# Attention with a fused feed-forward layer on one Trainium2 core: one softmax pass without a maximum, exponentials of 1536 columns, and an order of instructions made by a list scheduler

## The chip, the core and the metric

The kernel runs on one core of one Trainium2 chip. The metric is the device time of one execution in microseconds (us), from the first to the last instruction. Times that are compared come from the same call on the same chip unless the text says otherwise.

The kernels use five engines of the core. Each runs its own list of instructions, and they wait for one another at semaphores: TensorE (PE: matmuls; PEld: its weight loads), VectorE (DVE), ScalarE (ACT), GpSimd (POOL) and SyncE (SP, which issues the DMAs here). Matmul results land in PSUM, which the kernels use as 8 banks of 512 fp32 columns.

## The reference

```python
# S = 2048 tokens, D = 512, H = 32 heads of 16, F = 1792; all bf16
xn  = layernorm(x)
qkv = xn @ wqkv                                  # -> q, k, v per head
p   = softmax(q @ k.T * 0.25, axis=-1)           # 32 heads, 2048 x 2048 scores each
att = (p @ v) @ wo
ffn = (silu(xn @ w1) * (xn @ w3)) @ w2
out = x + att + ffn
```

Together the 32 heads have 32 x 2048 x 2048 scores. On 128 partitions that is 2048 tiles of 128 x 512, and every element of them goes through an exponential. ScalarE computes them all.

## The kernel before

The work is cut into 32 units: 4 blocks of 512 queries times 8 groups of 4 heads. Each unit is passed over twice. Pass 1 computes scores with queries on the partitions, and VectorE takes their maximum. The negated maximum is put into two spare rows of the query tile. Pass 2 computes the transposed scores, now shifted by the maximum, and ScalarE exponentiates them. A period of the program ("burst") holds two score matmuls of each pass:

```python
for i in range(2):                      # pass 1: banks 0..2 in turn
    b = (2 * p1 + i) % 3
    P.op("dve", lambda e: e.tensor_reduce(part[...], bank(b), AX.X, ALU.max), ...)
for i in range(2):                      # pass 2: banks 3..5 in turn, one 512-wide exp each
    r = 2 * p2 + i; b = 3 + r % 3
    P.op("act", lambda e: e.activation(PT[:, r % NPT, :], bank(b), ACTF.Exp, scale=SCALE), ...)
```

`PT` (exponentials, bf16) is multiplied with the values, which carry a column of ones, so bank 7 collects the weighted values and the row sums. Projections and the feed-forward layer ("dense tiles": 4 matmuls of 32 output columns side by side, called a group below) go through bank 6 in the remaining time. ScalarE copies nearly every dense result out of PSUM, in halves of 256 columns. Where a period has no dense group left, a filler multiplies zero weights into bank 7:

```python
if k == 0 and n < NB:
    filler(n)
```

## Time and profile before

| | |
|---|---|
| time, median of 3 | 1415.93 us (1413.53 to 1416.27) |
| VectorE busy | 1302.4 us, 92% |
| ScalarE busy | 1268.4 us, 89% |
| TensorE busy | 1042.1 us, 73% |
| granted TensorE clock, mean | 0.943 of full speed |

These lines of the page of the kernel before give the span, each engine's busy time with its share of the span and number of instructions, and the busy tenths in 40 equal slices; PEclk is the granted clock in tenths.

```profile
span 1417.8 us, 31821 instructions
PE 1042.1 (73%) x12357; PEld 270.8 (19%) x12357; DVE 1302.4 (92%) x2176; ACT 1268.4 (89%) x2709; POOL 251.0 (18%) x335
...
DVE  5999999999999999999999999999999999999801
ACT  4689999999999999989999999999999999999982
...
PEclk9998899999999999979999999999999999999998
...
DVE 42%; ACT 28%; PE 22%; issue 3%; POOL 2%; DMA 1%; SPq 0%; POOLq 0%; ACTq 0%; DVEq 0%
DVE part L778 42%; ACT PT L801 22%; PE ps L771 10%; PE ps L355 10%; PE ps L816 2%; ACT zg L374 1%; ACT QT L372 1%; ACT KT L390 1%; ACT ub L372 1%; ACT th L372 1%; PE ps L656 1%; DMA R<-Rrow 1%; ACT xnT L334 1%; POOL a L463 0%; ACT osb L372 0%
...
L778 DVE TENSOR_REDUCE part<-ps 128x1 f32<-128x512 f32 x2048 | 1267.3, 683 | 32.9 <-PE ps L771 21.6
L801 ACT ACTIVATE PT<-ps 128x512 bf16<-128x512 f32 x2048 | 1134.4, 619 | 87.0 <-PE ps L771 47.5
L771 PE MATMUL ps<-KT,QT 32*128 32x512 bf16 x2048 | 419.8, 403 | 288.9 <-DVE part L778 245.0
```

The two lines of percentages are the chain that ended last, by engine and by line. A group's line ends with its busy time, the mean duration of one in ns, and the idle time of its engine before it with what ended most of that. The reader should see two engines near 90%, a chain that changes sides between them, and a TensorE that waits 245 us for the reduction.

One more line is from the timeline of ScalarE near the end, where only pass 2 still runs (start, duration, engine, line, what, count):

```profile
1358.02 32.01 ACT L801 ACTIVATE PT<-ps 128x512 bf16<-128x512 f32 x58 [0.65 <-PE ps L771]
```

58 exponentials in 32.01 us are 0.552 us each. The line shows a wait of 0.65 us before the first of them and no gap between them.

### The profile page before, as it was taken

The page shows a single profiled execution, that of the slowest core. Times are in us where ns is not written, and L with a number is a line of the kernel's source. Part 1 is how long each engine was busy: PE and PEld are TensorE (multiplying, and loading weights), DVE is VectorE, ACT ScalarE, POOL GpSimd, SP SyncE. Part 2 cuts the span into 40 slices and gives each one's busy share as a digit, 9 for nine tenths or more (in the row PEclk, how much of TensorE's full clock was granted, in tenths as well). Part 3 has the DMA queues.
Part 4 walks back from the last instruction along what each step waited for, and adds up shares of the span by engine and source line. Part 5 has one row for each costly group of instructions (what it writes and reads, how often), then busy time and mean ns, then how long its engine had stood idle before and what let it go on. Part 6 is the DMA issues. An engine that isn't in the chain of part 4 may idle for free.

```text
span 1417.8 us, 31821 instructions
## 1 busy us (share of the span) xinstructions
PE 1042.1 (73%) x12357; PEld 270.8 (19%) x12357; DVE 1302.4 (92%) x2176; ACT 1268.4 (89%) x2709; POOL 251.0 (18%) x335
## 2 busy tenths in 40 slices
PE   4987777777777777777776777776777777777795
PEld 2321111111111111111111111111111111111121
DVE  5999999999999999999999999999999999999801
ACT  4689999999999999989999999999999999999982
POOL 5241010012122100112222011112221111112200
PEclk9998899999999999979999999999999999999998
DMA  9100111111111111110111111111111111011111
GB/s 215 28 12 4 11 6 13 6 13 20 18 19 13 17 17 17 18 20 16 21 20 21 17 17 17 5 29 20 21 21 20 17 17 6 13 25 20 6 6 20
DMA packets 80724, 29.85 MB, mean 21 GB/s; under 512 B 70336, under 2 KB 78528, under 8 KB 80576
## 3 DMA queue, kind: packets, MB, share of 16 engines
q1 hardware_dynamic: 80576, 27.81, 15.6%
q8 instruction: 101, 1.65, 0.5%
q14 instruction: 47, 0.39, 0.1%
HBM read 20.71 MB, written 2.10 MB: 16 GB/s over the span
## 4 chain that ended last, share of the span: by engine, by line
DVE 42%; ACT 28%; PE 22%; issue 3%; POOL 2%; DMA 1%; SPq 0%; POOLq 0%; ACTq 0%; DVEq 0%
DVE part L778 42%; ACT PT L801 22%; PE ps L771 10%; PE ps L355 10%; PE ps L816 2%; ACT zg L374 1%; ACT QT L372 1%; ACT KT L390 1%; ACT ub L372 1%; ACT th L372 1%; PE ps L656 1%; DMA R<-Rrow 1%; ACT xnT L334 1%; POOL a L463 0%; ACT osb L372 0%
## 5 line engine op out<-in xcount | busy, mean ns | idle before, releaser
L778 DVE TENSOR_REDUCE part<-ps 128x1 f32<-128x512 f32 x2048 | 1267.3, 683 | 32.9 <-PE ps L771 21.6
L801 ACT ACTIVATE PT<-ps 128x512 bf16<-128x512 f32 x2048 | 1134.4, 619 | 87.0 <-PE ps L771 47.5
L771 PE MATMUL ps<-KT,QT 32*128 32x512 bf16 x2048 | 419.8, 403 | 288.9 <-DVE part L778 245.0
L771 PE MATMUL ps<-QT,KT 32*128 32x512 bf16 x2048 | 418.4, 405 | 3.8 <-ACT PT L801 3.8
L771 PEld LDWEIGHTS ps<-KT,QT 32*128 32x128 bf16 x2048 | 107.4, 91 | 744.1 <-DVE part L778 743.2
L816 PE MATMUL ps<-PT,Vaug 128*17 128x512 bf16 x2048 | 211.7, 404 | 8.8 <-ACT U L372 8.4
L355 PE MATMUL ps<-xnT,w 128*32 128x512 bf16 x1792 | 162.2, 409 | 29.6 <-ACT QT L372 10.8
L656 PE MATMUL ps<-KT,zeros_t 128*17 128x512 bf16 x1400 | 138.3, 400 | 0.0
L771 PEld LDWEIGHTS ps<-QT,KT 32*128 32x128 bf16 x2048 | 96.9, 91 | 21.6 <-ACT PT L801 21.6
L463 POOL TENSOR_TENSOR a<-zg,ub 128x512 f32<-128x512 bf16 x56 | 64.7, 1155 | 75.7 <-ACT ub L372 75.5
L816 PEld LDWEIGHTS ps<-PT,Vaug 128*17 128x17 bf16 x2048 | 49.6, 87 | 138.2 <-issue 119.8
L786 POOL TENSOR_SCALAR negm<-mfin 128x16 f32<-128x16 f32 x32 | 6.6, 205 | 383.1 <-DVE mfin L783 383.1
L355 PE MATMUL ps<-w,hT 128*32 128x512 bf16 x896 | 73.5, 393 | 0.0
L465 POOL TENSOR_TENSOR hT<-a,t 128x512 bf16<-128x512 f32 x56 | 71.1, 1269 | 4.4
L461 POOL TENSOR_SCALAR t<-th 128x512 f32<-128x512 bf16 x56 | 34.8, 621 | 194.8 <-ACT th L372 193.8
L856 POOL TENSOR_TENSOR wk_on<-U,R 128x512 bf16<-128x512 f32 x16 | 20.3, 1268 | 256.7 <-DMA R<-Rrow 232.8
L856 POOL TENSOR_TENSOR on_b<-U,R 128x512 bf16<-128x512 f32 x16 | 20.3, 1270 | 225.9 <-DMA R<-Rrow 150.1
L355 PEld LDWEIGHTS ps<-xnT,w 128*32 128x32 bf16 x1792 | 39.8, 95 | 88.2 <-issue 81.8
L355 PE MATMUL ps<-xnT,wk_on 128*32 128x512 bf16 x512 | 50.0, 453 | 8.8 <-ACT xnT L334 3.6
L372 ACT ACTIVATE th<-zg 128x256 bf16<-128x256 bf16 x112 | 51.5, 460 | 0.5
L374 ACT ACTIVATE zg<-ps 128x256 bf16<-128x256 f32 x112 | 46.4, 414 | 3.7 <-PE ps L355 2.3
L355 PE MATMUL ps<-xnT,wq 128*32 128x512 bf16 x512 | 45.5, 396 | 3.6 <-ACT zg L374 3.6
(64 smaller groups left out, 475.1 us busy)
## 6 DMA issues: line engine op xcount, KB each, us to landing
w<-in_B_w_dram SPq DMA_DIRECT2D x112, 128.0 KB, 2.4
R<-Rrow SPq DMA_DIRECT2D x128, 32.0 KB, 3.4
x_sb<-in_A_x_dram SPq DMA_DIRECT2D x4, 512.0 KB, 7.9
out_dram<-osb SPq DMA_DIRECT2D x16, 128.0 KB
w<-in_B_w_dram SPq DMA_DIRECT2D x1, 1792.0 KB
hT<-in_A_wqkv_dram SPq DMA_DIRECT2D x3, 512.0 KB
QT<-Zs SPq DMA_DIRECT2D x64, 4.0 KB
wo<-in_A_wo_dram SPq DMA_DIRECT2D x4, 128.0 KB
```

Source lines behind the costliest of these rows:

```text
L355: ins = e.matmul(bank(bk)[32 * i:32 * i + 32, 0:ncols], make_lhsT(i), rhs_ap, start=start, stop=stop, tile_position=(0, 32 * i))
L372: P.op("act", lambda e: e.activation(dst_fn(h), src_fn(h), func), reads=reads, writes=writes)
L374: P.op("act", lambda e: e.activation(dst_fn(h), src_fn(h), func, scale=scale), reads=reads, writes=writes)
L461: P.op("pool", lambda e: e.tensor_scalar(t1[:, :], th[:, ss, :], 1.0, 1.0, ALU.mult, ALU.add), reads=[("th", ss)], writes=[("t1",)])
L463: P.op("pool", lambda e: e.tensor_tensor(a32[:, :], zg[:, ss, :], ub[:, ss, :], ALU.mult), reads=[("zg", ss), ("ub", ss)], writes=[("a32",)])
L465: P.op("pool", lambda e: e.tensor_tensor(hT[:, sc % 2, fc, :], a32[:, :], t1[:, :], ALU.mult), reads=[("a32",), ("t1",)], writes=[("hT", s ...
L656: ins = e.matmul(bank(7)[32 * j:32 * j + 17, :], zeros_t[:, 0:17], KT[:, 0, 0:512], start=False, stop=False, skip_group_check=True, tile_p ...
L771: ins = e.matmul(bank(b), lhsT, rhs, start=True, stop=True, tile_position=(rp, 0))
L778: P.op("dve", lambda e, qt=qt, j=j, kc=kc, b=b: e.tensor_reduce(part[:, qt, j, kc:kc + 1], bank(b), AX.X, ALU.max), reads=[("ps", b)], wri ...
L801: P.op("act", lambda e, b=b, r=r: e.activation(PT[:, r % NPT, :], bank(b), ACTF.Exp, scale=SCALE), reads=[("ps", b)], writes=[("PT", r % N ...
L816: ins = e.matmul(bank(7)[32 * j:32 * j + 17, :], Vaug[:, ktq, 4 * gq + j, :], PT[:, rj[j] % NPT, :], start=(ktq == 0), stop=(ktq == NT - 1 ...
L856: P.op("pool", lambda e: e.tensor_tensor(onorm[ob][:, gq, :], U[:, us, :], R[:, :], ALU.mult), reads=[("U", us)] + [("R", j_) for j_ in ra ...
```

## The change

Intent: drop the maximum, since the scores are small, and with it the whole first pass; make ScalarE's exponentials as wide as three banks; give ScalarE's copies to VectorE; and let a list scheduler, which runs at build time with a duration for each instruction, fix the order on every engine. The old two-pass program stays as a second program. On the chip the row sums are compared with 2^-20 and 2^60 and the value weights with 2^40; if the test fails, every engine runs the old program after the new one.

The core of the diff, with cuts marked:

```diff
+_LAT = 0.09
+class _Sched(_Prog):                     # list scheduler: op(..., dur=) has a modelled end
+    def op(self, eng, fn, reads=(), writes=(), dur=0.1, name=""):
+        op = _Prog.op(self, eng, fn, reads, writes, name)
+        return self._time(op, op.deps, dur, 0.18 if eng == "pe" else 0.0)
+    ...
+        a_cost = lambda n: 0.113 + 0.000835 * n      # ScalarE, n columns
+        d_cost = lambda n: 0.095 + 0.00104 * n       # VectorE
+    DG = 0.24                                        # four dense matmuls on TensorE
+    ...
+        def norm(t):
+            xs = t % 4
+            o = P.op("dve", lambda e: e.tensor_scalar(xn_sb[:, xs, :], x_sb[:, t, :], ...
+    ...
+            def emit():                              # w = 3 banks, two such buffers
+                q = P.op("act", lambda e: e.activation(
+                    PT[:, s0:s0 + w, :].rearrange("p a b -> p (a b)"),
+                    ps[:, 3 * buf * 512:(3 * buf + w) * 512],
+                    ACTF.Exp, scale=SCALE),
+                    reads=wr, writes=[("PT", r % NSL) for r in rs], dur=a_cost(512 * w))
+    ...
+                    elif try_score() or try_pv() or try_dense():     # TensorE's priorities
+                        moved = True
+    ...
+            reg = e.alloc_register("slow_" + name)
+            e.reg_load(reg, flag[0:1, 0:1])
+            with e.If(e.snap(reg) > 0):
+                ...
+                PM.emit_engine(name, e, sems[1][0], sems[1][1])     # the old program
```

The fast program has no fillers. Its exponentials number 683 (682 of 1536 columns and one of 1024). Scores have two buffers, banks 0 to 2 and 3 to 5; bank 6 takes dense tiles and bank 7 the value sums. Until the inputs are ready ("early") only the first score buffer is used.

## The prediction

> **What bounds the kernel now.** The page gives VectorE 92% busy, ScalarE 89%, TensorE 73% of a 1417.8 us span. The chain of waits runs 42% through the max reduction, 28% through ScalarE, 22% through TensorE. The groups view has 2048 reductions, 1267 us, and 2048 exponentials of 512 columns, 1134 us; around them ScalarE copies nearly every PSUM result (about 270 us). Two nearly full engines take turns as the limit, and one in-order TensorE feeds both: it waits 245 us for the reduction.
>
> **Removed.** All of pass 1: 2048 score matmuls and reductions, the max transposes with their copies and DMAs, 1400 filler matmuls. ScalarE's copies and GpSimd's gate products go to VectorE. VectorE falls from 1302 to about 170 us (some 240 operations of 0.62 us, plus norms), TensorE from 12357 matmuls to about 8600.
>
> **Left on ScalarE, the new bound.** In the tail of the old timeline, where only pass 2 runs, 58 exponentials take 32.0 us: 0.552 us for 512 columns. The Trainium skill ("ScalarE: Activation LUTs", What ACT_TABLE_LOAD costs) gives 0.833 ns per element and a fixed part; this trace agrees (256 columns 0.41 us, 512 columns 0.62 us, each alone). So 1536 columns should take 0.552 + 1024 x 0.833 ns = 1.405 us; 683 of them, 960 us. Widening alone is worth 170 us against 2048 x 0.552. Add 56 tanh, 31 us, and 14 transposed-input copies, 8 us.
>
> **Around it (estimates from durations in this trace).**
> - Start: first exponential at about 18 us (first burst now at 32).
> - Early phase: one score buffer, so some 20 exponentials also wait about 0.6 us for their scores: 12 us.
> - Tail: last values, three DMA hops for the division (the last took 6.5 us to land here), four short output tiles, output DMA: 20 us, against 27 now. The check mostly hides under it: 2 us.
> - Stalls where the static order differs from the chip: about 25 us.
>
> Sum: 960 + 31 + 8 + 18 + 12 + 20 + 2 + 25, about 1075; I shade it to 1065, since a timed list scheduler made the order. Row sums are far inside the check's limits (scores of standard deviation near 1.3 over 2048 keys), so the fallback is not run.
>
> **Prediction: 1065 us, range 1030 to 1115. Faster by over 2%: 0.97; within 2%: 0.01; slower: 0.02** (only if the fallback runs, near 2400 us).
>
> **What would show each step.** ScalarE at 93% or more of the span; one group of 683 exponentials at about 1.40 us per step; the chain of waits over 75% in them; VectorE under 20% busy; TensorE 60 to 70%; ScalarE's idle time before exponentials, released by TensorE, 20 to 50 us in all.
>
> **What would make it wrong.** (1) Without fillers TensorE's granted clock (0.943 now) may drop in stretches that hold only scores and values, as the skill ("TensorE: Matmul & The Clock Gate", Part 1) warns of idle. Slow bursts in this trace take 0.61 instead of 0.39 us, a dense group 0.43 instead of 0.22. Scores alone still fit into 1.4 us; interleaved with dense tiles they would not, and ScalarE would starve: I expect a mean clock of 0.75 to 0.95. A clock near 0.5 throughout would cost 50 us or more. (2) A read across three PSUM banks may be slower than linear. (3) The single bank for dense tiles may hold TensorE behind a late evacuation, and so the next scores. (4) The dense work of a quarter waits for the last division of the quarter before, so it may pile up at the end.

## The result, and the profile after

| | before | after |
|---|---|---|
| time, median | 1416.01 us (4 runs) | 1023.31 us (4 runs, 1019.11 to 1024.02) |
| ratio | | 0.7225, 95% interval 0.7208 to 0.7242 |
| VectorE busy | 1302.4 us, 92% | 203.1 us, 20% |
| ScalarE busy | 1268.4 us, 89% | 959.1 us, 94% |
| TensorE busy | 1042.1 us, 73% | 803.3 us, 79% |
| mean granted clock | 0.943 | 0.824 |

The time lies below the predicted range (1030 to 1115 us). The output is correct.

These are the same lines of the page of the changed kernel.

```profile
span 1022.1 us, 19380 instructions
PE 803.3 (79%) x8641; PEld 221.6 (22%) x8641; DVE 203.1 (20%) x347; ACT 959.1 (94%) x755; POOL 61.0 (6%) x81
...
DVE  7742233310001222100001222200001122210012
ACT  2799999999999999999999999999999999999991
...
PEclk9999999975579999855559999955558999975578
...
ACT 77%; PE 15%; DVE 3%; DMA 2%; issue 2%; SPq 0%; DVEq 0%
ACT f_PT L1464 74%; PE ps L1192 9%; PE ps L1454 4%; ACT f_th L1291 3%; PE ps L1491 2%; DMA f_wv<-in_A_wqkv_dram 1%; DVE f_KT L1203 1%; DMA f_Lc<-f_U 1%; DVE f_hT L1305 0%; DMA f_R<-f_Rrow 0%; DVE f_xn_sb L1096 0%; DVE f_t L1295 0%; PE ps L1214 0%; DVE f_QT L1203 0%; DVE f_osb L1352 0%
...
L1464 ACT ACTIVATE f_PT<-ps 128x1536 bf16<-128x1536 f32 (+1 forms) x683 | 940.6, 1661 | 24.2 <-PE ps L1454 24.0
L1454 PE MATMUL ps<-f_QT,f_KT 32*128 32x512 bf16 x2048 | 319.6, 462 | 139.5 <-ACT f_PT L1464 136.1
```

The chain now runs through ScalarE, with 24 us of idle time before exponentials that scores ended. The clock has long stretches at half speed, marked 5 in PEclk. (The mean of 1661 ns is no step: the record of an exponential may start while the one before still runs. Steps must be taken from ends.)

The ends of consecutive exponentials, taken one by one from the two traces, give this table. It holds only pairs with nothing else between them on ScalarE.

```
kernel, exponentials                  pairs   step, us (number of pairs)
before, 512 wide, all                 1508    0.488 to 0.492 (1024 pairs); the rest mostly 0.69 to 0.71 (311) and 0.76 (65)
before, 512 wide, after 1358 us         57    0.488 and 0.612 in turn; mean 0.551
after, 1536 wide                       621    1.340 to 1.345 (589 pairs); median 1.343
```

This table is where the prediction failed. The 0.552 us is the mean of a step that ScalarE takes by itself (0.488) and one in which it waits for scores (0.612), because two exponentials share one burst of scores and three banks don't let the next burst start in time. The score matmuls of the old tail (TensorE's timeline) show it:

```profile
1359.77 0.39 PE L771 MATMUL ps<-QT,KT 32*128 32x512 bf16 x2 [0.71 <-ACT PT L801]
...
1360.87 0.39 PE L771 MATMUL ps<-QT,KT 32*128 32x512 bf16 x2
...
1361.97 0.39 PE L771 MATMUL ps<-QT,KT 32*128 32x512 bf16 x2 [0.16 <-ACT PT L801]
...
1363.07 0.39 PE L771 MATMUL ps<-QT,KT 32*128 32x512 bf16 x2
```

A burst comes every 1.10 us, which is 0.488 + 0.612. In the trace the burst at 1360.87 starts 0.05 us after an exponential has ended at 1360.82, so it waited for that bank. The first exponential on its scores is released only at 1361.29, just as the exponential before ends at 1361.30. The timeline of ScalarE shows no gap because records overlap: an exponential that doesn't wait starts 0.10 us before the one before ends, and one that waits starts 0.015 us after it. ScalarE's own step is 0.488 us for 512 columns and 1.343 us for 1536. The line through these two has 0.835 ns per column and 0.061 us fixed, half of the 0.125 us that the prediction carried into every one of the 683.

The largest part of the steady idle time looks like this. It is the timeline of the changed kernel around a query tile at half clock.

```profile
257.15 0.61 PE L1454 MATMUL ps<-f_QT,f_KT 32*128 32x512 bf16 x3 [0.20 <-ACT f_PT L1464]
...
257.69 0.61 PE L1491 MATMUL ps<-f_PT,f_Vaug 128*17 128x512 bf16 x4
...
258.09 1.92 PE L1192 MATMUL ps<-f_xnT,f_wq 128*32 128x512 bf16 x16
...
259.94 1.03 PE L1454 MATMUL ps<-f_QT,f_KT 32*128 32x512 bf16 x6
...
260.60 4.13 ACT L1464 ACTIVATE f_PT<-ps 128x1536 bf16<-128x1536 f32 x3 [0.81 <-PE ps L1454]
```

The four groups of the query tile (16 matmuls) take 1.92 us, where the scheduler allowed 4 x 0.24. The next scores stand behind them, and ScalarE starves for 0.8 us. Over the steady part (53 to 1001 us) ScalarE idles 15.9 us in all.

The start and the early phase hold the rest. These lines are VectorE and GpSimd just before and after the first exponential.

```profile
20.26 4.09 DVE L1096 TENSOR_SCALAR f_xn_sb<-f_x_sb,f_lnr,f_lnb 128x512 bf16<-128x512 bf16 x2
...
20.37 3.51 POOL L1142 MEMSET f_wo<- 128x4096 bf16 x1
```

Two normalisations that take 0.7 us together elsewhere take 4.09 us while GpSimd clears the output weights; the first alone takes 3.77 us. The Trainium skill ("SBUF — State Buffer", SBUF: two separate sides) says that VectorE in some modes and GpSimd hold a common pair of ports exclusively for a whole instruction. The trace agrees: the first normalisation ends 0.15 us after the 3.51 us of the clearing, and the second follows at its normal 0.39 us. (The record of the first starts 0.11 us before that of the clearing, so these records don't tell which of the two got the ports first.)

### The profile page after: what moved, and what is told of

Read it like the earlier page. It is cut to its first block, busy times and chain, and to the rows that moved or that the text cites. A ratio compares the mean times of both kernels' runs of the same rounds, so it can differ in the third digit from the quotient of the medians.

```text
span 1022.1 us, 19380 instructions
## 1 busy us (share of the span) xinstructions
PE 803.3 (79%) x8641; PEld 221.6 (22%) x8641; DVE 203.1 (20%) x347; ACT 959.1 (94%) x755; POOL 61.0 (6%) x81
## 3 DMA queue, kind: packets, MB, share of 16 engines
q1 hardware_dynamic: 80080, 27.54, 21.5%
## 4 chain that ended last, share of the span: by engine, by line
ACT 77%; PE 15%; DVE 3%; DMA 2%; issue 2%; SPq 0%; DVEq 0%
ACT f_PT L1464 74%; PE ps L1192 9%; PE ps L1454 4%; ACT f_th L1291 3%; PE ps L1491 2%; DMA f_wv<-in_A_wqkv_dram 1%; DVE f_KT L1203 1%; DMA f_Lc<-f_U 1%; DVE f_hT L1305 0%; DMA f_R<-f_Rrow 0%; DVE f_xn_sb L1096 0%; DVE f_t L1295 0%; PE ps L1214 0%; DVE f_QT L1203 0%; DVE f_osb L1352 0%
## 5 line engine op out<-in xcount | busy, mean ns | idle before, releaser
L1464 ACT ACTIVATE f_PT<-ps 128x1536 bf16<-128x1536 f32 (+1 forms) x683 | 940.6, 1661 | 24.2 <-PE ps L1454 24.0
L1454 PE MATMUL ps<-f_QT,f_KT 32*128 32x512 bf16 x2048 | 319.6, 462 | 139.5 <-ACT f_PT L1464 136.1
L1491 PE MATMUL ps<-f_PT,f_Vaug 128*17 128x512 bf16 x2048 | 239.7, 459 | 0.7 <-DVE f_U L1508 0.7
L1454 PEld LDWEIGHTS ps<-f_QT,f_KT 32*128 32x128 bf16 x2048 | 68.6, 94 | 434.8 <-ACT f_PT L1464 387.9
L1192 PE MATMUL ps<-f_xnT,f_w 128*32 128x512 bf16 x1792 | 129.3, 381 | 38.8 <-DVE f_t L1295 26.6
L1491 PEld LDWEIGHTS ps<-f_PT,f_Vaug 128*17 128x17 bf16 x2048 | 50.1, 88 | 156.6 <-issue 148.6
L1192 PE MATMUL ps<-f_w,f_hT 128*32 128x512 bf16 x896 | 64.8, 398 | 2.8 <-DVE f_osb L1352 1.6
L1192 PEld LDWEIGHTS ps<-f_xnT,f_w 128*32 128x32 bf16 x1792 | 42.7, 95 | 86.9 <-issue 61.2
L1192 PE MATMUL ps<-f_xnT,f_wq 128*32 128x512 bf16 x512 | 47.0, 484 | 7.2 <-DVE f_t L1295 5.6
L1291 ACT ACTIVATE f_th<-ps 128x512 f32<-128x512 f32 x56 | 49.2, 878 | 1.4 <-PE ps L1192 1.4
```

Of the source, the lines that this page charges most:

```text
L1192: ins = e.matmul(bank(bk)[32 * i:32 * i + 32, 0:ncols], make_lhsT(i), rhs_ap, start=start, stop=stop, tile_position=(0, 32 * i))
L1291: q = P.op("act", lambda e: e.activation(th[:, ss, :], bank(bk), ACTF.Tanh, scale=0.5), reads=[("ps", bk)], writes=[("th", ss)], dur=a_cos ...
L1454: ins = e.matmul(bank(b), l_, r_, start=True, stop=True, tile_position=(rp, 0))
L1464: q = P.op("act", lambda e: e.activation(PT[:, s0:s0 + w, :].rearrange("p a b -> p (a b)"), ps[:, 3 * buf * 512:(3 * buf + w) * 512], ACTF ...
L1491: ins = e.matmul(bank(PV)[32 * j:32 * j + 17, :], Vaug[:, kt, 4 * g + j, :], PT[:, (4 * m + j) % NSL, :], start=(kt == 0), stop=(kt == NT ...
```

## The experiments

The theories at the start were these.
- A: the step of an exponential was mis-sized, because its fixed part is 0.061 us. The rival R1 keeps 0.125 us and gives another reason for cheap wide reads.
- B: the steady stalls come from query tiles at half clock.
- C: the start is late because value tiles block TensorE.
- D and E, formed later, are about where the rest of the gain comes from.

The ratios are against the kernel before.

### Width of the exponential

exp_512 and exp_768 cut each exponential into three or two.

```diff
-  q = P.op("act", lambda e: e.activation(PT[.., s0:s0+w, ..], ps[three banks], Exp),
-           reads=wr, writes=[("PT", r % NSL) for r in rs], dur=a_cost(512 * w))
+  for h in range(3):                     # exp_768: range(2), 768 columns
+      q = P.op("act", lambda e, h=h: e.activation(PTf[:, h*step:(h+1)*step], ps[...], Exp),
+               reads=wr, writes=[("PT", r % NSL) for r in rs], dur=a_cost(step))
```

> The changed kernel with every 1536-wide exponential cut into three of 512 columns; scores, order and buffers stay. Theory A (the fixed part of one exponential is about 62 ns, read from back-to-back steps of 0.488 us for 512 columns in the old trace and 1.343 us for 1536 in the new one; the prediction's 0.552 us came from a stretch where ScalarE also waited for scores): 1365 more instructions x 62 ns = +85 us, about 1108 us. Rival R1 (the fixed part is 125 ns, as the prediction took, and a wide read over three banks is cheaper for another reason): +170 us, about 1193 us.

> The same with two exponentials of 768 columns (the cut lies inside a bank). Theory A: 683 x 62 ns = +42 us, about 1065 us, step 0.70 us. Rival R1: +85 us, about 1108 us. If only the number of instructions counts, exp_512 adds twice what this adds.

Measured: exp_512 1284.78 us (ratio 0.9068) with a wrong result; exp_768 1154.51 us (0.8153), correct. Both are far slower than either theory allowed. Their steps show why: exp_512 has 592 steps of 0.488 us and 1365 of 0.629 us; exp_768 has 572 of 0.700 to 0.702 and 682 of about 0.842 us. 1365 and 682 are the numbers of pieces that follow another piece of the same exponential. My edit named all three banks and slots for each piece, so the program made each piece wait for ScalarE's own semaphore of the piece before, and that wait costs 0.141 us. Steps without it are 0.488 and 0.701 us, and 0.701 - 256 x 0.835 ns is 0.487: one line through all three widths.

The wrong result has its own cause. A replay of the order in which the build emits operations shows it: the normalised input tiles have four slots, and `norm(t)` has no condition that the transpose of tile t - 4 was emitted. In the change only the modelled times keep that order. With the slower exponentials, tile 13 was emitted before the transpose of tile 9. The trace of exp_512 agrees: that normalisation starts at 34.9 us, and the transpose of tile 9 ends at 35.8. The check for races sees nothing, since every access waits for the one emitted before it.

exp_512_free mends both: exact banks and slots, and conditions for reused slots.

```diff
-  P.post("dve", lambda t=t: norm(t), ready=..., prio=1)
+  P.post("dve", lambda t=t: norm(t), ready=..., prio=1,
+         cond=lambda t=t: t < 4 or ("TR", t - 4) in done)
+  # the same for the copies U and R of the division of unit u - 2 and u - 1
+  for h in range(w):
+      q = P.op("act", ... PT[:, s0 + h, :], bank 3*buf+h ..., reads=[wr[h]], writes=[("PT", s0 + h)])
```

> exp_512 once more, with two mistakes of that run mended: each 512-wide exponential names only its own bank and its own slot, so that none waits on its own engine for the one before (two of three did, at 0.629 us a step against 0.488), and the normalised input tiles and the divisions wait for the slot they overwrite, which the change itself leaves to the modelled times. Result correct. Theory A: 1365 more instructions x 61 ns = +83 us over 1022, 1100 to 1112 us, all steps near 0.488. Rival R1: +170 us. If it is still wrong, the order of the input tiles was not the cause.

Measured: 1102.03 us (ratio 0.7794, interval 0.7776 to 0.7812), correct; 1950 of 1986 steps are 0.488 to 0.492 us. That is 80 us above the changed kernel (1020 to 1023 us), against 83 by theory A and 170 by R1. R1 is out. Widening is worth 80 us, not the 170 us of the prediction.

### Copies back on ScalarE, and the fallback by force

copies_act moves the copies of keys, queries and values to ScalarE; forced_fallback sets `L_HI = 2.0 ** 4`, so that the check must fail.

> The changed kernel with the copies of keys, queries and values (80 tiles of 512 columns) put back from VectorE to ScalarE. If ScalarE is the bound through nearly the whole span, each copy adds its step of 0.49 us: +39 us, less a few for the 21 early ones that fall into ScalarE's idle time: 1050 to 1062 us. Rival (the limit is the handoff of scores by TensorE): ScalarE has room, below +10 us.

> The upper limit of the row-sum check lowered to 16, so the check fails on purpose and the two-pass program runs after the fast one. The result stays correct and the time is near the sum of both, 1022 + 1416 = 2440 us. If the check were not wired to the branch, the time would stay at 1022 us.

Measured: copies_act 1047.29 us (0.7400), about 25 us more than the changed kernel and a little under the expected range. ScalarE's share rose to 96%. Of 561 steps between exponentials 556 stayed at 1.343 us; the copies of the early phase fell into idle time, and the stalls at query tiles shrank from 0.92 to 0.38 us, which the expectation had left out. So ScalarE is the bound through most of the span: of the 39 us of steps given to it (80 x 0.49), about 25 were paid, and the rest went into idle time that was there before (24 of the 80 copies start before 53 us). The result was wrong for the reason above: the replay shows tiles 12 to 15 emitted before the transposes of 8 to 11, and the trace has the same order. The work is the same.

forced_fallback took 2426.9 us in one run and was correct. The check is wired to the branch, and failing it costs about the sum of both programs (1022 + 1416 = 2438 us).

### Stalls and clock

slow_dense sets `DG = 0.45`; fillers adds zero-weight matmuls wherever the schedule leaves TensorE idle.

```diff
   elif try_score() or try_pv() or try_dense():
       moved = True
+  elif not st["early"] and st["sc"] < NGR and pvb[0] <= P.t and st["pv"] % NT:
+      ...   # four matmuls, zero weights, added to the open sums in bank 7, dur=0.24
```

> The changed kernel once more, as the yardstick for the small effects of this call: 1019 to 1024 us, ratio 0.7225.

> The scheduler is told that a dense group of four matmuls takes 0.45 us instead of 0.24. Theory B (the 15 or so stalls of 0.9 us in the steady part come from the four groups of a query tile, which take 1.9 us at half clock in front of the next scores, where the schedule allowed 0.96): the groups are spread over two or more exponentials, the stalls go, -10 to -15 us, with the clock still low (about 0.8). Rival B2 (the stalls come from the low clock itself, whatever the order): no change within 3 us.

> Filler matmuls (zero weights added to the open value sums) where the schedule leaves TensorE idle, to hold the clock up. Theory B: clock above 0.95, query tiles take 1.05 us, the stalls of 0.9 us go, -10 to -15 us, unless the fillers themselves stand in front of scores. Rival B2 says the same here; so this run with slow_dense tells order from clock. If the clock costs nothing anywhere: no change or slower.

Measured: after_again 1020.13 us (0.7217); slow_dense 1030.75 us (0.7281), wrong result; fillers 1011.39 us (0.7148, interval 0.7132 to 0.7164), correct.

slow_dense doesn't tell order from clock. Its clock rose to 0.904, where about 0.8 was expected. The constant also slowed the early phase (first exponential at 27.6 us instead of 21.1) and left one stall of 6.9 us at 76.8 us, where scores stood behind several tiles of keys and queries in a row; and at query tiles stalls of 0.51 and some 0.2 us remained, since two groups still fit between scores in the model. Its result is wrong because tiles 12 to 15 overtook again, and because in the replay a division's factors were overwritten by the next unit's before use (in the trace the load of the next factors is issued before the multiplication at 3 of 32 units). Fillers held the clock at 0.993, and the stalls of 0.9 us were gone. The gain was 9 us, a little less than expected, because fillers themselves now stood before scores and left many stalls of 0.12 to 0.18 us. The trace agrees with the gain: ScalarE's stalls after 53 us, counted beyond each instruction's own step, fell from 14.9 us in after_again to 5.8. So the low clock cost about 1% here, through the query tiles. Whether another order would have avoided these stalls at the low clock is not shown. This is PEclk of fillers:

```profile
PEclk9999999999999999999999999999999999999997
```

### The start

v_late lets value tiles begin only after the first scores.

```diff
-  crit = [(0, i, x) for i, x in enumerate(order)]
+  crit = [(1 if x.name[0] == "V" else 0, i, x) for i, x in enumerate(order)]
```

> Value tiles may start only after the first group of scores is issued. In the trace TensorE stands at 12 us waiting for the load of the value weights, with the transposes of input tiles 2 and 3 behind two cold value tiles, and the first exponential starts at 20.8 us. Theory C: the first exponential comes 5 us or so earlier, and the whole gains 2 to 5 us. Rival (the early phase is bound by VectorE and TensorE together until 53 us): the first exponential comes earlier, the end does not move, within 2 us.

Measured: 1019.62 us (0.7202) against 1020.13. The first exponential came at 16.2 us instead of 21.1, and the end did not move. The rival holds: until about 53 us other things bound the early phase (the 4.09 us above are still there).

### Where the rest of the gain comes from

one_pass_old is the kernel before with pass 1 and the maximum taken out. one_pass_old_dve moves its copies to VectorE too.

```diff
-  p1 = n if n < NPB else None
+  p1 = None                    # no pass 1, so no maximum and no shift
-  LAG = BU + 8
+  LAG = 28
-  assert ("QTP", u2) in done, ...
+  assert ("QT", u2) in done and ("KT", g2, kt // 4) in done, ...
+  # one_pass_old_dve only:  evac_on_dve = [True]
```

> The kernel before with pass 1 and the maximum taken out and nothing else: 512-wide exponentials, three score banks, the old order by periods, copies on ScalarE. Theory D (ScalarE and its handoff take over at once as the bound): 1024 pairs at 0.488 + 0.611 us as in the old tail, 1126 us, plus copies of 256 columns that do not fit into the handoff waits, about 120 us, plus start 70 and tail 27 us: about 1340 us, a gain of only 75 us although VectorE loses 1267 us of work. Rival (the reductions were the bound by themselves): about 1200 us or less.

> The same with the copies moved from ScalarE to VectorE (all but those of the keys). Theory D: 1126 + tanh 30 + start 70 + tail 27 us, about 1255 us; what then is left to the changed kernel (about 230 us) is the width of the exponentials with double-buffered groups of three banks, and the start. If the handoff were not the limit, 2048 x 0.488 = 1000 us would show instead: about 1130 us.

Measured: one_pass_old **1487.92 us**, ratio 1.0544, so slower than the kernel before although VectorE lost 1267 us of work; one_pass_old_dve 1379.43 us (0.9749). Theory D fell. The clock was 0.663 and 0.753. This is the stretch from 400 to 440 us of one_pass_old (columns: stretch, length, busy time and count of PE, PEld, DVE, ACT and POOL, granted clock, DMA share, GB/s):

```profile
400.00:440.00 40.00, 37.21 (x244) 6.37 (x240) 0.25 (x1) 34.77 (x75) 9.75 (x9) 0.54 0.17 21
```

TensorE is busy 37.2 of 40 us, yet it completes only 244 matmuls, and its clock stays at half. In the same stretch the kernel before does more matmuls in less time:

```profile
400.00:440.00 40.00, 29.04 (x332) 7.25 (x328) 38.90 (x65) 38.09 (x85) 8.10 (x10) 0.91 0.16 19
```

To tell the clock from the handoff, one_pass_warm and one_pass_dve_warm add work: they keep the two score matmuls of pass 1 in each period, into banks that nobody reads.

```diff
-  if p1 is None and n >= NPB + 2:        # the old kernel did this in its tail only
+  if p2 is not None:
       for i in range(2):
           mms.append((i, KT[32*j:32*j+32, 0, 0:128], KT[32*j:32*j+32, 0, 0:512], 32*j))
```

> one_pass_old with two more score matmuls in every period, into banks that nobody reads, so that TensorE's work is as in the kernel before but no reduction waits on it. Theory E (the low clock made one_pass_old slow: at half clock TensorE is full): clock above 0.9, 1320 to 1370 us. Rival E2 (the handoff over three banks and the copies on ScalarE cost it, whatever the clock): more work for TensorE makes it no faster, 1480 us or more.

> The same for one_pass_old_dve. Theory E: clock above 0.9, 1240 to 1280 us, the pair of exponentials stepping 0.488 + 0.611 us. Rival E2: about 1380 us.

Measured: one_pass_warm **1330.30 us** (0.9399), one_pass_dve_warm 1265.84 us (0.8946), both correct, with clocks of 0.963 and 0.973. 2048 useless matmuls made the kernels 158 and 114 us faster. The same stretch of one_pass_warm:

```profile
400.00:440.00 40.00, 32.15 (x392) 7.34 (x388) 0.25 (x1) 38.47 (x77) 1.85 (x2) 0.96 0.11 9
```

392 matmuls now take less time than 244 did. Theory E holds for both. In one_pass_dve_warm 1024 steps between exponentials are 0.488 us and 829 of the other 869 are 0.61 us, the handoff again. With the clock held up, theory D's sums (1340 and 1255 us) come within 11 us of what is measured; the clock was what they had left out.

So the gain divides into steps. The first two were measured at a clock of 0.96 and 0.97, the last two at 0.81 and 0.82; holding the clock of the changed kernel up with fillers gave 9 us more. The sizes hold for this order of the steps. They are differences of medians of different calls, whose medians of the kernel before differ by under 4 us:

```
                                                          us      gain
kernel before                                           1415
one pass, TensorE kept warm        (one_pass_warm)      1330        85
copies (not of keys) to VectorE    (one_pass_dve_warm)  1266        64
list order, double-buffered scores (exp_512_free)       1102       164
exponentials of 1536 columns       (after)              1022        80
```

The "one pass" of the title gives 85 us of 393, and by itself in the old order it gives less than nothing. The largest step is the one in which ScalarE no longer waits for its scores: 829 steps of 0.61 us that become 0.488 are worth about 829 x 0.12 = 100 us of it (an estimate from the steps above). The two traces divide the 164 us further: the first exponential starts at 64.7 us in one_pass_dve_warm and at 21.9 in exp_512_free, which is 43 us; the tail after the last one is 7 us shorter; and the stretch from the first exponential to the last is 115 us shorter. No run separates the double buffer from the list order.

### The check

> The changed kernel without the flag's register loads, branches and second program (the flag is still computed). By the prediction 2 us faster, 1018 to 1020 us where the full one has 1020 to 1023; if the branch and the last waits hide nothing, 3 to 5 us faster.

> The changed kernel again, as the yardstick for no_check on the same chip: 1019 to 1024 us.

Measured: no_check 1018.76 us (0.7206, interval 0.7181 to 0.7230), after_third 1023.47 us (0.7236, interval 0.7214 to 0.7258). The intervals of the ratios overlap, but their five times don't overlap: 1016.71 to 1021.67 us against 1022.69 to 1024.45, with means 4.3 us apart. The traces give the place. From the end of the last exponential to the end of the span no_check takes 18.5 us, and the three profiles of the changed kernel 21.5, 21.6 and 22.4. So the check costs 3 to 4 us and not 2.

In the trace of the changed kernel the flag is written at 1005.0 us, long before the end. SyncE loads it at 1017.7, after its last output DMA, and its branch ends at 1018.4. The last output data have landed at 1019.4, but SyncE's waits for the DMA semaphores begin only at 1020.9, 2.5 us after the branch, and follow one by one until 1021.7. In no_check they begin 0.05 us after the last output DMA is issued. TensorE's branch alone takes 3.9 us, ending at 1018.7, before SyncE is done.

### A faster version

best_b takes what the runs taught: fillers only where the modelled exponential has 0.7 us left, the true cost of an exponential in the scheduler, late value tiles, early copies on ScalarE where it is idle, the clearing of the output weights at 70 us, and the missing conditions.

```diff
-  a_cost = lambda n: 0.113 + 0.000835 * n
+  a_cost = lambda n: 0.061 + 0.000835 * n
+  elif ... P.free["act"] > P.t + 0.7 ...: filler
```

> The changed kernel with: fillers only where the modelled exponential still has 0.7 us to run; the exponential's cost in the scheduler corrected to 0.061 us + 0.835 ns per column; value tiles after the first scores; the clearing of the output weights on GpSimd moved from 20 us to 70 us, since in the trace two normalisations on VectorE took 4.09 us under it instead of 0.7; early copies on ScalarE where it is idle; and the missing waits for the overwritten slots. Stalls of 15 us in the steady part and 3 to 8 us of the early phase go: 995 to 1008 us, correct. If the small stalls in front of scores seen with fillers stay, about 1008 to 1012 us.

Measured: **999.83 us** (996.97 to 1000.35, ratio 0.7072, interval 0.7057 to 0.7086), correct. These are lines of its page.

```profile
span 998.6 us, 23622 instructions
PE 836.3 (84%) x10765; PEld 238.5 (24%) x10765; DVE 194.7 (19%) x339; ACT 960.4 (96%) x763; POOL 61.4 (6%) x82
...
PEclk9999999999999999999899999999989999998998
...
ACT 91%; PE 4%; issue 2%; DMA 1%; DVE 1%; SPq 0%; POOL 0%; DVEq 0%
```

Between its first exponential and the last, ScalarE loses about 6 us beyond the instructions' own steps, against about 29 us in the changed kernel. From VectorE's timeline, two normalisations take their normal time again:

```profile
18.83 0.73 DVE L1099 TENSOR_SCALAR f_xn_sb<-f_x_sb,f_lnr,f_lnb 128x512 bf16<-128x512 bf16 x2
```

The parts of best_b were not measured one by one, apart from fillers (in another form) and v_late. v_late still has the 4.09 us, so moving the clearing is what removed them.

## Why the prediction was right or wrong

The predicted sum, before it was shaded to 1065, against what the trace of the changed kernel has (stalls are counted beyond each instruction's own step from end to end, which adds about 0.1 us per stall to the gaps between records):

| term of the prediction | predicted, us | measured, us |
|---|---|---|
| 683 exponentials | 960 | 917 (683 x 1.343) |
| 56 tanh | 31 | 27 (56 x 0.489) |
| 14 input copies | 8 | 7 |
| first exponential at | 18 | 20.8 |
| early waits and stalls | 12 + 25 | about 29 (10 before 53 us, 19 after) |
| tail and check | 20 + 2 | 21.5 |
| sum | 1075 | 1022 |

**What failed.** The step that failed is "58 exponentials take 32.0 us: 0.552 us for 512 columns", and with it "1536 columns should take 0.552 + 1024 x 0.833 ns = 1.405 us; 683 of them, 960 us". The mechanism was right and the slope was right; the term that was mis-sized is the fixed part, 0.125 us where 0.061 was measured. It was read from a stretch in which every second exponential waited 0.12 us for scores. Of the 53 us that the sum was too high, 43 are this term. The experiments with 512 and 768 columns and the changed kernel with 1536 have 0.488, 0.701 and 1.343 us. The other 10 us are small errors that partly cancel. The 25 us for stalls had no working behind them, so that they came near is luck, and the shading by 10 us had no number behind it either.

The same mistake stands in "Widening alone is worth 170 us": it is worth 80. It also stands in the scheduler of the change, whose cost of 0.113 us + 0.835 ns per column is 1.396 us for 1536.

**What was right.**
- The new bound is ScalarE, at 94% where the prediction says "93% or more". The chain passes 74% in the exponentials, just under the "over 75%" of the prediction.
- VectorE is at 19.9% (203.1 us, where about 170 us was predicted), the edge of "under 20%". The fallback did not run.
- ScalarE's idle time before exponentials released by TensorE, 24 us, lies in the predicted 20 to 50. The start, the tail and the early terms came within a few us.
- The clock fell to 0.824, inside 0.75 to 0.95, and as feared the stalls come where dense tiles stand before scores (about 9 us by the run with fillers).

**What I had not seen.** TensorE's busy share came to 79% and not 60 to 70%, because the same matmuls last longer at half clock (their records average 462 ns for scores, against 393 in best_b with its clock of 0.98). The prediction put the gain down to removed work and wider exponentials; the runs show that the largest step of it is removed waiting for scores.

## What to carry to other kernels

Before you scale an instruction's time to another width, take its step from the ends of consecutive instructions and look at the distribution: a mean of 0.55 us that alternates between 0.488 and 0.612 holds a wait. Before you remove work from an engine, ask what that work did for its clock: here taking away half of the score matmuls made the kernel 5% slower, and putting useless ones back made it 6% faster than the start. An order made from modelled times needs an explicit condition for each reused buffer; a change of one constant gave wrong results here that the check for races did not see.

## What the Trainium skill lacked or had wrong

- "ScalarE: Activation LUTs" (What ACT_TABLE_LOAD costs) gives 186 ns + 0.833 ns per element and an overlap of about 93 ns between consecutive instructions, so 93 ns fixed when they follow each other, without saying where the operands lie. These runs show 0.061 us fixed and 0.835 ns per column from PSUM to bf16: 0.488 us for 512 columns, 0.701 for 768, 1.343 for 1536. Another page, "Perfetto Trace Analysis" (Optimizing Scalar/DVE Operations), gives about 51 ns of overhead per ScalarE instruction for PSUM, which is nearer.
- No page says what a wait on ScalarE's own previous instruction costs: 0.141 us here (steps of 0.629 against 0.488, and 0.842 against 0.701).
- "TensorE: Matmul & The Clock Gate" (Part 1 and the table of why it matters) ties the low clock to idle gaps of about 3 us. In one_pass_old the clock was 0.54 over 40 us in which TensorE was busy 37.2 us, and 0.96 in one_pass_warm with 32.2 us busy and 392 matmuls instead of 244. From 62 to 1455 us of one_pass_old no idle gap of TensorE is longer than 0.87 us, and the granted clock still drops to half 28 times. Busy time in the profile doesn't say whether the clock will be granted; what the hardware counts instead, these runs do not show.
- No page has the cost of a branch over a long unexecuted program; the skill times only a branch by itself. In this trace it took 3.9 us on TensorE and 0.05 to 0.07 us on the other engines, but on those the next recorded instruction starts 2.4 to 2.9 us after the branch.
